# Windowed attention in whole units of eight heads, with scores merged into 128 columns, ahead of two feed-forward layers

## Chip, cores and metric

One Trainium2 chip, one core. The metric is the device time of one execution in microseconds (us). Matrix products run on TensorE (PE), everything else on VectorE (DVE), ScalarE (ACT) and GpSimd (POOL); loads and stores are issued by SyncE (SP).

## What is computed

Three layers follow each other, on 1152 tokens (2 sequences of 576) of 512 numbers:

```python
# 1: attention, 8 heads of 64, window of 128 keys, a bias by distance for each head
scores = scale * np.matmul(q, k.transpose(0, 1, 3, 2))
mask = (rel >= 0) & (rel < window)            # rel = query position - key position
scores = np.where(mask, scores + slopes * -abs(rel), -1e9)
attn = softmax(scores); x = attn @ v          # heads side by side: x is [1152, 512]
# 2: four experts
for e in range(4):
    out += p[:, e:e+1] * (np.maximum(x @ w1[e], 0.0) @ w2[e])   # 512 -> 1024 -> 512
# 3: one more layer
h = out @ w_in                                 # 512 -> 2048
result = (h * np.cos(h)) @ w_out               # 2048 -> 512
```

## The kernel before

Every float32 operand of layers 2 and 3 is split into a high and a low part (`hi`, `lo`), and a product is three passes of matmuls over them. Layers 2 and 3 are done in 12 groups g of 512 hidden features: 0 to 7 are the experts (two each), 8 to 11 the last layer; between groups 7 and 8, at the turn, `flip` transposes the layer's output on PE into the next x. Of the 1152 tokens two thirds go in pairs (`pair`, seven products of 384 columns with sums of operands, T1 to T4, S1 to S4, that `transform` and `first_sums` prepare on ACT, DVE and POOL), the last third by `plain`. `layer2(g, t)` multiplies one tile of 128 tokens by the group's second weights, twelve matmuls, and DVE adds the result into `acc`.

Attention works on 10 units (b, i), the blocks of queries of the two sequences: the first of each has 64 rows, the others 128. A unit is done in two halves of four heads, so there are 20 steps, and step k does the scores of half k (`att_scores`), the sums and normalisation of half k-1, the transposes of half k-3 and the value products of half k-4 (`LAG`). A block of queries sees its own block of keys and the one before, so scores are up to 256 wide: PE writes them to PSUM, DVE adds the bias `bm` and takes the minimum (L362, with the scores' sign turned), ACT takes the exponential (L367) and their sum, DVE inverts it (L376, L377), POOL multiplies (L383), PE transposes both key blocks of each head, eight transposes for a half (L405), DVE and ACT copy them out as `pt` (L415, L417), and PE multiplies by the values of both blocks (L433). A finished unit's x is split (`split_x`, L333, for the last third of the tokens) or transformed (L278 to L313, for the others).

All of this stands in the program in the order in which it is written (`tc.manual_schedule()`), and every engine runs its own instructions in that order. The function `fill(k, s)` puts other work between attention's parts: one `next(jobs)` is a piece of the splitting of weights (an ACT copy and a POOL subtraction of 128x512, or two POOL sums `sm`), `plain` halves are the first group's products, `move(n)` takes n stages of a waiting transform. When a job is through with a raw weight tile it issues the load of the next one (`loads_ahead`, L145, two buffers `raw`) on SP, where the loads of the units stand too (`load_units_to`, L120 to L122).

PSUM has eight banks. During attention `ps1` has two of them for products, the scores three, the transposes two, x one. Afterwards `mm` has six, and `bank()` takes `ps1` for every fourth product. In the groups, `run` goes through `steps(g)`: each entry is a product with the number of stages, jobs and conversions of the last layer's weights (`cv`) that follow it, and at a group's end all waiting transforms are finished.

Of the kernel before, what the change touches and what calls it, by code (L numbers as in the profile page):

```python
# [24 lines left out]
WIN = 128  # L25
# [20 lines left out]
LAG = 3  # L46


@with_exitstack
def tile_kernel(ctx, tc, qT, kT, v, probs, w1, w2, w_in, w_out, out):  # L50
# [13 lines left out]
    ps1 = pool("ps1", bufs=2, space=PSUM)  # L64
# [7 lines left out]
    ptp = ap("ptp", bufs=4)  # L72
    stp = ap("stp", bufs=6)
    ps_s = ap("ps_s", bufs=3, space=PSUM)
# [5 lines left out]
    scr = ppool.tile([128, 4, 256], F32, name="scr", tag="p")  # L80
    bm = mkp.tile([128, H, 256], BF16, name="bm")

    def constants():
        rel_i, rel, msk = scr[:, 0].bitcast(I32), scr[:, 1], scr[:, 2]
        nc.gpsimd.iota(rel_i, pattern=[[-1, 256]], base=WIN, channel_multiplier=1)
        nc.vector.tensor_copy(rel, rel_i)
        nc.gpsimd.memset(msk, 0.0)
        big = -8.0e9
        nc.gpsimd.affine_select(
            out=msk, in_=msk, pattern=[[-1, 256]], compare_op=ALU.is_ge, fill=big,  # L90
            base=WIN, channel_multiplier=1,
        )
        nc.gpsimd.affine_select(
            out=msk, in_=msk, pattern=[[1, 256]], compare_op=ALU.is_ge, fill=big,
            base=-1, channel_multiplier=-1,
        )

        for h in range(H):
            slope = 2.0 ** (-8.0 * (h + 1) / H)
            nc.vector.scalar_tensor_tensor(  # L100
                out=bm[:, h, :], in0=rel, scalar=-8.0 * slope, in1=msk,
                op0=ALU.mult, op1=ALU.add,
            )
        make_identity(nc, ident)


    k_t, q_t, v_t = {}, {}, {}

    def load_unit(b, i):
# [13 lines left out]
        q_t[b, i], v_t[b, i] = qt, vt  # L123

# [215 lines left out]
    def att_scores(u, g):  # L340
# [3 lines left out]
        wid = s0 + n - k0  # L344
        c0 = WIN if i == 0 else 256 - wid
        ps = [ps_s.tile([128, 2, 256], F32, name="s_ps", tag="s_ps") for _ in range(2)]
        for m in range(2):
            for hh in range(2):
                r = slice(64 * hh, 64 * hh + 64)
                nc.tensor.matmul(  # L350
                    ps[hh][:n, m, :wid], q_t[u][r, 2 * g + m, :n],
                    k_t[b][r, 2 * g + m, k0 : s0 + n], start=True, stop=True,
                )
        p = ppool.tile([128, 4, 256], F32, name="p", tag="p")
        nmax = stp.tile([128, 4], F32, name="nmax", tag="nmax")
        den = dens[:, (2 * units.index(u) + g) % 4]
        rec = stp.tile([128, 4], F32, name="rec", tag="rec")
        for m in range(2):
            for hh in range(2):
# [3 lines left out]
                    out=p[:n, k, :wid], in0=ps[hh][:n, m, :wid], in1=bm[:n, h, c0 : c0 + wid],  # L363
# [4 lines left out]
                    out=p[:n, k, :wid], in_=p[:n, k, :wid], func=AF.Exp, scale=-1.0,  # L368
                    bias=nmax[:n, k : k + 1], accum_out=den[:n, k, 0:1],
                )  # L370
        state[u, g] = p, den, rec, wid
# [7 lines left out]
    def att_normalise(u, g):  # L379
        n = UNITS[u[1]][1]  # L380
        p, den, rec, wid = state[u, g]
        for s in (slice(0, 4),) if u[0] == 0 else (slice(0, 2), slice(2, 4)):
            nc.gpsimd.tensor_tensor(  # L383
                out=p[:n, s, :wid], in0=p[:n, s, :wid],
                in1=rec[:n, s].unsqueeze(2).to_broadcast([n, s.stop - s.start, wid]), op=ALU.mult,
            )
        state[u, g] = p

    def key_blocks(i):
        o = 0  # L390
# [291 lines left out]
    with tc.manual_schedule():  # L682
# [13 lines left out]
        def fill(k, s):  # L696
# [5 lines left out]
            if (k, s) == (11, 0):  # L702
                routing()
# [145 lines left out]
```

## Time and profile before

| | us |
|---|---|
| median of 3 runs | 669.71 |
| lowest, highest | 668.44, 672.1 |
| the profiled execution | 668.45 |
| its span in the trace | 666.7 |
| PE, weight loads on PE (PEld) busy | 645.6, 568.7 |
| DVE, ACT, POOL busy | 432.8, 335.9, 367.6 |

The profile shows one execution. Attention takes the first 88.2 us of the span, the pairs of group 0 begin there; the turn lies around 440 to 490, the four groups of the last layer after it. In a timeline, us of start are counted from the span's start, and a bracket gives the engine's idle time just before the instruction and what ended it. Instructions of one engine overlap at their ends, so the distance between two starts, not the duration, is what one costs in a row.

### The profile page before, as it was taken

Reading aid. Unit: us, or ns where it says so; the run is one execution under the profiler, and the core shown is the slowest. Engines: PE = TensorE matmul, PEld = TensorE weight load, DVE = VectorE, ACT = ScalarE, POOL = GpSimd, SP = SyncE. Lnnn points to the kernel's source line nnn. Section 1 sums busy time; section 2 is a strip of 40 time slices with the busy share of each in tenths; the row PEclk is TensorE's granted clock in tenths of the full one; section 3 lists DMA queues with packets and bytes.
Section 4 is the critical chain, followed back from the end, with each engine's and each line's share of the span. In section 5 each row is a group of like instructions: output and inputs, shape, how many; then the busy total and the mean of one; then the engine's idle time right before and its main releaser. Section 6 shows DMA issues by size and latency. Waiting matters only on the chain.

```text
span 666.7 us, 9755 instructions
## 1 busy us (share of the span) xinstructions
PE 645.6 (97%) x3516; PEld 568.7 (85%) x3516; DVE 432.8 (65%) x842; ACT 335.9 (50%) x768; POOL 367.6 (55%) x346
## 2 busy tenths in 40 slices
PE   8989899999999999999999999999799999999997
PEld 5677698998998998988988988988788988988976
DVE  7676776878668578589578562647663563563562
ACT  6878644453344354354343341346684674584560
POOL 3977729356265175183282381465468558558530
PEclk8999999999999999999999999999899999999999
DMA  9162114435417335245236130030101101202002
GB/s 262 41 204 83 32 33 138 130 112 200 128 35 225 106 101 185 79 139 193 80 131 200 32 121 7 32 96 0 33 0 64 65 0 63 65 0 64 17 31 94
DMA packets 39727, 60.40 MB, mean 91 GB/s; under 512 B 5632, under 2 KB 22016, under 8 KB 39680
## 3 DMA queue, kind: packets, MB, share of 16 engines
q1 hardware_dynamic: 39680, 59.80, 28.2%
q8 instruction: 27, 0.44, 0.3%
q14 instruction: 20, 0.16, 0.1%
HBM read 49.04 MB, written 10.75 MB: 90 GB/s over the span
## 4 chain that ended last, share of the span: by engine, by line
PE 78%; DVE 7%; ACT 7%; POOL 4%; issue 2%; DMA 1%; SPq 0%; ACTq 0%; DVEq 0%; POOLq 0%
PE o_ps L631 39%; PE o_ps L537 21%; PE o_ps L565 13%; PE s_ps L350 2%; DVE u L509 2%; ACT r L507 2%; ACT u L506 2%; PE x_ps L433 1%; POOL p L383 1%; POOL w1t L130 1%; PE t_ps L405 1%; POOL hpair L130 1%; DVE o_ps L580 1%; DVE xs L130 1%; DVE u L515 1%
## 5 line engine op out<-in xcount | busy, mean ns | idle before, releaser
L631 PE MATMUL o_ps<-w2t,hpair 128*128 128x512 f32 x864 | 207.3, 392 | 4.3 <-POOL hpair L130 4.1
L631 PEld LDWEIGHTS o_ps<-w2t,hpair 128*128 128x128 f32 x864 | 160.7, 188 | 38.3 <-POOL hpair L130 5.8
L537 PE MATMUL o_ps<-xs,w1t 128*128 128x384 f32 x1008 | 182.5, 338 | 3.9 <-DVE c L580 1.8
L537 PEld LDWEIGHTS o_ps<-xs,w1t 128*128 128x128 f32 x1008 | 177.1, 189 | 7.6 <-DVE c L580 3.1
L130 POOL TENSOR_TENSOR w2t<-raw,w2t 128x512 fp32r<-128x512 f32 x48 | 66.2, 1394 | 82.1 <-ACT w2t L185 82.1
L130 POOL TENSOR_TENSOR w1t<-raw,w1t 128x512 fp32r<-128x512 f32 x48 | 65.0, 1364 | 83.2 <-ACT w1t L155 83.0
L565 PE MATMUL o_ps<-xq,w1t 128*128 128x384 f32 x576 | 110.3, 338 | 0.0
L565 PEld LDWEIGHTS o_ps<-xq,w1t 128*128 128x128 f32 x576 | 101.6, 188 | 3.3
L631 PE MATMUL o_ps<-w2t,h 128*128 128x512 f32 x432 | 103.3, 392 | 0.0
L631 PEld LDWEIGHTS o_ps<-w2t,h 128*128 128x128 f32 x432 | 80.7, 188 | 16.1 <-issue 0.2
L130 POOL TENSOR_TENSOR w1t<-sm,w1t 128x512 fp32r<-128x512 f32 x48 | 64.6, 1356 | 41.9 <-ACT w1t L155 35.1
L509 DVE SCALAR_TENSOR_TENSOR u<-r,u 128x384 f32<-128x384 f32 x48 | 34.6, 726 | 51.7 <-ACT r L507 51.7
L130 POOL TENSOR_TENSOR hpair<-u,hpair 128x384 fp32r<-128x384 f32 x32 | 33.6, 1066 | 42.3 <-ACT hpair L517 42.3
L245 ACT ACTIVATE cr<-cr 128x512 f32<-128x512 f32 x32 | 21.6, 675 | 43.4 <-DVE cv L239 43.4
L367 ACT ACTIVATE p<-p,nmax 128x256 f32<-128x256 f32 (+2 forms) x80 | 36.2, 454 | 13.0 <-DVE nmax L362 12.8
L646 DVE SCALAR_TENSOR_TENSOR accpair<-o_ps,pr,accpair 128x512 f32<-128x512 f32 x42 | 31.3, 745 | 17.3 <-PE o_ps L631 17.3
L233 ACT ACTIVATE cr<-cr 128x512 int32<-128x512 uint32 x32 | 21.6, 675 | 40.7 <-DMA cr<-w_in 25.3
L524 ACT ACTIVATE hpair<-o_ps 128x384 fp32r<-128x384 f32 x48 | 23.4, 488 | 36.6 <-DVE o_ps L580 35.9
L155 ACT ACTIVATE w1t<-sm 128x512 fp32r<-128x512 f32 x48 | 30.0, 627 | 20.3 <-POOL sm L130 20.3
L525 DVE SCALAR_TENSOR_TENSOR hpair<-o_ps,hpair 128x384 fp32r<-128x384 f32 x48 | 26.6, 555 | 20.3 <-ACT hpair L524 20.3
L383 POOL TENSOR_TENSOR p<-p,rec 128x512 f32<-128x512 f32 (+5 forms) x30 | 32.6, 1102 | 9.5 <-DVE rec L377 5.6
L239 DVE SCALAR_TENSOR_TENSOR cv<-cr,cv 128x512 int32<-128x512 int32 x32 | 35.1, 1097 | 1.1
(100 smaller groups left out, 821.3 us busy)
## 6 DMA issues: line engine op xcount, KB each, us to landing
raw<-w SPq DMA_DIRECT2D x32, 512.0 KB, 3.7
cr<-w_in SPq DMA_DIRECT2D x16, 512.0 KB, 4.6
cr<-w_out SPq DMA_DIRECT2D x16, 512.0 KB, 4.5
wi<-cv SPq DMA_DIRECT2D x16, 256.0 KB, 3.6
wo<-cv SPq DMA_DIRECT2D x16, 256.0 KB, 2.3
raw<-wi SPq DMA_DIRECT2D x8, 512.0 KB, 3.5
raw<-wo SPq DMA_DIRECT2D x8, 512.0 KB, 3.5
qt<-qT SPq DMA_DIRECT2D x8, 256.0 KB, 4.9
```

The costliest lines, as they stand in the source:

```text
L130: eng.tensor_tensor(out=out, in0=a, in1=b, op=ALU.subtract)
L155: nc.scalar.activation(out=hi[:, s], in_=src[:, s], func=AF.Copy)
L239: nc.vector.scalar_tensor_tensor(out=a, in0=hw, scalar=-0x40000000, in1=o, op0=ALU.bitwise_and, op1=ALU.bitwise_or,)
L367: nc.scalar.activation(out=p[:n, k, :wid], in_=p[:n, k, :wid], func=AF.Exp, scale=-1.0, bias=nmax[:n, k : k + 1], accum_out=den[:n, k, 0:1],)
L383: nc.gpsimd.tensor_tensor(out=p[:n, s, :wid], in0=p[:n, s, :wid], in1=rec[:n, s].unsqueeze(2).to_broadcast([n, s.stop - s.start, wid]), op ...
L509: nc.vector.scalar_tensor_tensor(out=u, in0=r, scalar=MAGIC, in1=u, op0=ALU.subtract, op1=ALU.subtract)
L524: nc.scalar.activation(out=hi, in_=src, func=AF.Relu)
L525: nc.vector.scalar_tensor_tensor(out=lo, in0=src, scalar=0.0, in1=hi.bitcast(F32), op0=ALU.max, op1=ALU.subtract)
L537: nc.tensor.matmul(ps, w(a, k, m), xs[:, bb, b, m], start=(start and m == 0 and (a, bb) == PASSES[0]), stop=(stop and m == 1 and (a, bb) = ...
L565: nc.tensor.matmul(ps, w(a, 2 * (q % 2) + d // 2, d % 2), xq[:, bb, d], start=(d == 0 and (a, bb) == PASSES[0]), stop=(d == ND - 1 and (a, ...
L631: nc.tensor.matmul(ps, h0[:, a, f, t * 128 : (t + 1) * 128] if t < NQ else hpair[:, a, f, (t - NQ) * 128 : (t - NQ + 1) * 128], w_t[2, g, ...
L646: nc.vector.scalar_tensor_tensor(out=o, in0=ps, scalar=s, in1=o, op0=ALU.mult, op1=ALU.add)
```

## The change

A step is now a whole unit: the scores of both halves, then in between the rest of older units. In program order, for unit k: scores of both halves; sums and normalisation of half 0; value products of unit k-2; `fill`; transposes of half 0 of unit k-1; `fill`; sums and normalisation of half 1; transposes of half 1 of unit k-1; `fill`.

A query sees exactly 128 keys, and of each column of the two key blocks only one is in the window: the one before for a key that is later in its block than the query is in its own. So `copy_predicated` (DVE) lays the older block's scores over the newer one's where the mask `later` says so, and the bias, exponential, normalisation and transposes are done on 128 columns. For the value products a masked copy `po` (pt times `own`) is made, and the result is `ahead` times pt plus `vd` times po, where `ahead` are the older block's values and `vd` the difference of the two, a POOL subtraction for each unit (`values`).

```diff
-    ps1 = pool("ps1", bufs=2, space=PSUM)
+    ps1 = pool("ps1", bufs=1, space=PSUM)
-    ptp = ap("ptp", bufs=4)
+    ptp = ap("ptp", bufs=2)
+    vdp = ap("vdp", bufs=3)
-    ps_s = ap("ps_s", bufs=3, space=PSUM)
+    ps_s = ap("ps_s", bufs=4, space=PSUM)
...
     def load_unit(b, i):
+        if i == 1:
+            nc.sync.dma_start(out=va[64:], in_=v[b, :64, :])
+    def values(b, i):
+        ahead = va if i == 1 else v_t[b, i - 1]
+        vd = vdp.tile([128, DM], F32, name="vd", tag="vd")
+        nc.gpsimd.tensor_tensor(out=vd, in0=v_t[b, i], in1=ahead, op=ALU.subtract)
+        v_d[b, i] = ahead, vd
...
     def att_scores(u, g):
+        if i:
+            for hh in range(2):
+                nc.vector.copy_predicated(
+                    ps[hh][:n, :, 128 + c0 :], later.bitcast(U32)[:n, :, c0:], ps[hh][:n, :, c0:128]
+                )
...
-                    out=p[:n, k, :wid], in0=ps[hh][:n, m, :wid], in1=bm[:n, h, c0 : c0 + wid],
+                    out=p[:n, k, :n], in0=ps[hh][:n, m, 128 : 128 + n], in1=bm[:n, int(i > 1), h, :n],
...
     def att_normalise(u, g):
-        for s in (slice(0, 4),) if u[0] == 0 else (slice(0, 2), slice(2, 4)):
...
+        nc.gpsimd.tensor_tensor(
+            out=p[:n, :, :n], in0=p[:n, :, :n],
+            in1=rec[:n].unsqueeze(2).to_broadcast([n, 4, n]), op=ALU.mult,
+        )
+        if g == 0 and u[1]:
+            values(*u)
     def att_transpose(u, g):
+        for k in range(4):
+            nc.tensor.transpose(tp[:n, k, :n], p[:n, k, :n], ident[:n, :n])
+        nc.scalar.activation(out=pt[:n, :, :n], in_=tp[:n, :, :n], func=AF.Copy)
+            nc.vector.tensor_tensor(
+                out=po, in0=tp, in1=own.unsqueeze(1).to_broadcast([128, 4, 128]), op=ALU.mult
+            )
     def att_pv(u, g):
+                nc.tensor.matmul(o, ahead[:, hs], pt[:, k], start=True, stop=False)
+                nc.tensor.matmul(o, more[:, hs], po[:, k], start=False, stop=True)
...
     def attention(fill):
+        for k in range(n):
+            load_units_to(k + 2)
+            at(k, att_scores, 0)
+            at(k, att_scores, 1)
+            at(k, att_sums, 0)
+            at(k, att_normalise, 0)
+            at(k - 2, att_pv, 0)
+            at(k - 2, att_pv, 1)
             fill(k, 0)
+            at(k - 1, att_transpose, 0)
             fill(k, 1)
+            at(k, att_sums, 1)
+            at(k, att_normalise, 1)
+            at(k - 1, att_transpose, 1)
             fill(k, 2)
...
     def bank():
-        return ps1 if mm is None or count[0] % 4 == 0 else mm
+        return ps1 if mm is None or count[0] % 8 == 0 else mm
...
         def fill(k, s):
-            if s == 0 and 4 <= k < 20:
+            if s and 2 <= k < 10:
                 next(jobs)
-            move(24 if (k, s) == (23, 2) else 2 * (s > 0))
+            move(24 if (k, s) == (11, 1) else 4 if k >= 10 else 2)
...
-    mm = pool("mm", bufs=6, space=PSUM)
+    mm = pool("mm", bufs=7, space=PSUM)
...
     def steps(g):
-            yield layer2(g, 1), 2, 2 if turn else int(not last), 2
-            yield layer2(g, 2), 2, 2 if turn else int(not last), 2
+            yield layer2(g, 1), 2, 2 if turn else int(early), 2
+            yield layer2(g, 2), 2, 2 if turn else int(early), 2
...
-        njobs = 0 if last else 4 if turn else 6 if early else 10
+        njobs = [1] * 10
...
+        elif not last:
+            njobs = [0, 1, 2, 2, 1, 2, 1, 1, 1, 1]
     def run(groups):
-                move(2)
+                move(2 if ncv or stages != 1 else 1)
-            while moved:
-                move(24)
```

The constants change with it (`later`, `own`, the two biases `bm`), the plain halves of group 0 move to units 6 to 9, and three tiles `layer2(0, 0..2)` to the steps behind the last unit. For groups 0 to 7 the number of jobs at each step stays.

On SP, the loads around the first weight load of the second kind (raw of 128x2x512, which waits for a buffer that the sums `sm` give back); the three rows behind it are the loads of unit 6. Before:

```order
L120 DMA qt<-qT 128x4x64
L121 DMA kt<-kT 128x4x64
L122 DMA vt<-v 64x512
L145 DMA raw<-w 128x2x512
L120 DMA qt<-qT 128x512
L121 DMA kt<-kT 128x4x128
L122 DMA vt<-v 128x512
```

And after:

```order
L141 DMA qt<-qT 128x4x64
L142 DMA kt<-kT 128x4x64
L143 DMA vt<-v 64x512
L176 DMA raw<-w 128x2x512
L141 DMA qt<-qT 128x512
L142 DMA kt<-kT 128x4x128
L143 DMA vt<-v 128x512
L147 DMA va<-v 64x512
```

The order is the same; only the load of `va` came in behind.

On DVE, the end of attention: the transform of the last unit (tx, xk and xs) and behind it the first step of the first pair product, u. acc is the eviction of a second-layer tile. Before:

```order
L644 TENSOR_SCALAR acc_129<-o_ps,pr 128x512
L130 TENSOR_TENSOR xs<-xk,xs 128x2x128
L130 TENSOR_TENSOR xk<-xk,tx 128x2x128
L130 TENSOR_TENSOR xs<-xk,xs 128x2x128
L130 TENSOR_TENSOR tx<-x_ps,xk 128x256
L130 TENSOR_TENSOR tx<-x_ps,tx 128x256
L130 TENSOR_TENSOR xk<-x_ps,xk 128x256
L130 TENSOR_TENSOR xs<-xk,xs 128x2x128
L130 TENSOR_TENSOR xs<-tx,xs 128x2x128
L130 TENSOR_TENSOR xs<-xk,xs 128x2x128
L644 TENSOR_SCALAR acc_129<-o_ps,pr 128x512
L580 TENSOR_TENSOR u_1328<-o_ps,p_1319 128x384
```

After:

```order
L682 TENSOR_SCALAR acc_135<-o_ps,pr 128x512
L161 TENSOR_TENSOR tx<-x_ps,xk 128x256
L161 TENSOR_TENSOR tx<-x_ps,tx 128x256
L161 TENSOR_TENSOR xk<-x_ps,xk 128x256
L161 TENSOR_TENSOR xs<-xk,xs 128x2x128
L161 TENSOR_TENSOR xs<-tx,xs 128x2x128
L161 TENSOR_TENSOR xs<-xk,xs 128x2x128
L161 TENSOR_TENSOR xk<-xk,tx 128x2x128
L161 TENSOR_TENSOR xs<-xk,xs 128x2x128
L682 TENSOR_SCALAR acc_135<-o_ps,pr 128x512
L618 TENSOR_TENSOR u_1288<-o_ps,p_1279 128x384
```

The last eviction stands behind the whole transform of the last unit in both; the rest of the transform before it has moved ahead of the second-last eviction.

On POOL, the turn: xs<-accpair are low parts of the transformed x, h and hpair low parts of the hidden layer, w2t and w1t those of weights. Before:

```order
L130 TENSOR_TENSOR xs<-accpair,xs 128x2x128 x2
L130 TENSOR_TENSOR h_128<-u,h_128 128x384
L130 TENSOR_TENSOR w2t<-raw,w2t 128x512 x2
L130 TENSOR_TENSOR h_128<-u,h_128 128x384
L130 TENSOR_TENSOR hpair<-u,hpair 128x384 x4
L130 TENSOR_TENSOR w1t<-raw,w1t 128x512 x2
L130 TENSOR_TENSOR hpair<-u,hpair 128x384 x2
L130 TENSOR_TENSOR w1t<-raw,w1t 128x512
L130 TENSOR_TENSOR hpair<-u,hpair 128x384 x2
L130 TENSOR_TENSOR w1t<-raw,w1t 128x512
```

After:

```order
L161 TENSOR_TENSOR xs<-accpair,xs 128x2x128
L161 TENSOR_TENSOR h_134<-u,h_134 128x384
L161 TENSOR_TENSOR w2t<-raw,w2t 128x512 x2
L161 TENSOR_TENSOR xs<-accpair,xs 128x2x128
L161 TENSOR_TENSOR h_134<-u,h_134 128x384
L161 TENSOR_TENSOR hpair<-u,hpair 128x384 x4
L161 TENSOR_TENSOR w1t<-raw,w1t 128x512 x2
L161 TENSOR_TENSOR hpair<-u,hpair 128x384 x4
L161 TENSOR_TENSOR w1t<-raw,w1t 128x512
L161 TENSOR_TENSOR h_134<-u,h_134 128x384
L161 TENSOR_TENSOR w1t<-raw,w1t 128x512
```

The last low part of x has moved behind the two w2t steps, and the third w1t step, which stood between hpair's low parts, behind all of them.

## Rows read from the trace of the kernel before

**Rows 1.** Windows: us, busy us (count) PE PEld DVE ACT POOL, clock, DMA, GB/s

```profile
0.00:88.20 88.20, 80.27 (x685) 60.18 (x686) 62.50 (x270) 65.96 (x231) 60.30 (x67) 0.98 0.40 122
...
476.50:480.20 3.70, 3.70 (x12) 3.70 (x13) 2.19 (x4) 2.71 (x6) 3.29 (x3) 0.55 0.15 46
```

**Rows 2.** Chain of waits, 0 to 160: start us, us, what

```profile
32.15 1.42 POOL sm L130 x2
...
33.59 0.38 SPq L145
...
34.55 4.30 DMA kt<-kT
...
42.10 1.02 PE x_ps L433 x16
...
62.25 1.06 PE s_ps L350 x8
...
63.32 1.02 PE t_ps L405 x8
...
85.41 2.94 PE o_ps L631 x12
```

**Rows 3.** Timeline of DVE, attention: start us, us, instruction, idle before

```profile
19.51 0.42 DVE L362 CUSTOM_DVE_ANT_0 p<-s_ps,bm 128x256 f32<-128x256 f32 x1
...
26.59 0.69 DVE L130 TENSOR_TENSOR xq<-x_ps,xq 128x512 fp32r<-128x512 f32 x1 [1.87 <-ACT xq L333]
27.19 0.42 DVE L362 CUSTOM_DVE_ANT_0 p<-s_ps,bm 128x256 f32<-128x256 f32 x1
...
28.57 0.16 DVE L376 TENSOR_REDUCE rec<-dens 128x4 f32<-128x8 f32 x1
...
28.85 0.66 DVE L415 COPY pt<-t_ps 128x512 f32<-128x512 f32 x1
...
33.78 0.20 DVE L362 CUSTOM_DVE_ANT_0 p<-s_ps,bm 64x64 f32<-64x64 f32 x1
...
40.09 0.34 DVE L362 CUSTOM_DVE_ANT_0 p<-s_ps,bm 128x192 f32<-128x192 f32 x1
...
63.45 0.42 DVE L362 CUSTOM_DVE_ANT_0 p<-s_ps,bm 128x256 f32<-128x256 f32 x1
...
91.25 0.75 DVE L644 TENSOR_SCALAR acc<-o_ps,pr 128x512 f32<-128x512 f32 x1
```

**Rows 4.** Groups by line and shape: busy us, mean ns, idle before

```profile
L383 POOL TENSOR_TENSOR p<-p,rec 128x512 f32<-128x512 f32 x12 | 12.4, 1057 | 0.7 <-DVE rec L377 0.7
...
L367 ACT ACTIVATE p<-p,nmax 128x256 f32<-128x256 f32 x48 | 23.8, 498 | 6.5 <-DVE nmax L362 6.4
...
L367 ACT ACTIVATE p<-p,nmax 64x64 f32<-64x64 f32 x16 | 5.3, 335 | 4.8 <-DVE nmax L362 4.8
...
L130 DVE TENSOR_TENSOR accpair<-accpair,tx 128x256 f32<-128x256 f32 x3 | 2.6, 859 | 0.1
...
L130 DVE TENSOR_TENSOR tx<-x_ps,xk 128x256 f32<-128x256 f32 x3 | 1.3, 425 | 0.7 <-ACT xk L286 0.7
```

**Rows 5.** Timeline of ACT, unit 4 and the end of attention

```profile
25.96 0.59 ACT L333 ACTIVATE xq<-x_ps 128x512 fp32r<-128x512 f32 x1
27.65 0.51 ACT L367 ACTIVATE p<-p,nmax 128x256 f32<-128x256 f32 x1 [1.10 <-DVE nmax L362]
...
85.52 0.60 ACT L286 ACTIVATE xk<-x_ps 128x512 f32<-128x512 f32 x1
```

**Rows 6.** Waits of PE, 430 to 667: us in total, times, longest

```profile
PE o_ps L631 <- POOL hpair L130: 4.1, 4, 1.4
...
PE o_ps L537 <- ACT p L586: 1.7, 1, 1.7
```

**Rows 7.** Timeline of PE at the turn

```profile
476.50 3.91 PE L537 MATMUL o_ps<-xs,w1t 128*128 128x384 f32 x12 [1.31 <-DVE c L580]
```

**Rows 8.** Timeline of POOL at the turn

```profile
475.99 2.52 POOL L130 TENSOR_TENSOR w2t<-raw,w2t 128x512 fp32r<-128x512 f32 x2
```

More of the change, by code (lines that the diff above doesn't have):

```diff
@@ new lines, in tile_kernel @@
+    own = mkp.tile([128, 128], F32, name="own")
+    va = mkp.tile([128, DM], F32, name="va")
+    bm = mkp.tile([128, 2, H, 128], BF16, name="bm")
+    def constants():
+        rel_i = own.bitcast(I32)
+        nc.gpsimd.iota(rel_i, pattern=[[-1, 128]], base=0, channel_multiplier=1)
+        nc.gpsimd.memset(later, 0.0)
+        nc.gpsimd.affine_select(
+            out=later, in_=later, pattern=[[0, 2], [-1, 128]], compare_op=ALU.is_ge, fill=float(WIN),
+            base=0, channel_multiplier=1,
+        )
@@ L86, in constants @@
         nc.vector.tensor_copy(rel, rel_i)
-        nc.gpsimd.memset(msk, 0.0)
-        big = -8.0e9
+        nc.vector.tensor_tensor(out=rel, in0=rel, in1=later[:, 0], op=ALU.add)
+        nc.gpsimd.memset(edge, 0.0)
         nc.gpsimd.affine_select(
-            out=msk, in_=msk, pattern=[[-1, 256]], compare_op=ALU.is_ge, fill=big,
-            base=WIN, channel_multiplier=1,
-        )
+            out=edge[:, :64], in_=edge[:, :64], pattern=[[-1, 64]], compare_op=ALU.is_ge, fill=-8.0e9,
+            base=0, channel_multiplier=1,
+        )
@@ new lines, in constants @@
+        for e in range(2):
+            for h in range(H):
+                slope = 2.0 ** (-8.0 * (h + 1) / H)
+                if e == 0:
+                    nc.vector.scalar_tensor_tensor(
+                        out=bm[:, e, h], in0=rel, scalar=-8.0 * slope, in1=edge,
+                        op0=ALU.mult, op1=ALU.add,
+                    )
+                else:
+                    nc.gpsimd.tensor_scalar(
+                        out=bm[:, e, h], in0=rel, scalar1=-8.0 * slope, scalar2=None, op0=ALU.mult
+                    )
+            if e == 0:
+                make_identity(nc, ident)
@@ L93, in constants @@
+        nc.gpsimd.memset(va[:64], 0.0)
+        nc.gpsimd.memset(own, 1.0)
         nc.gpsimd.affine_select(
-            out=msk, in_=msk, pattern=[[1, 256]], compare_op=ALU.is_ge, fill=big,
-            base=-1, channel_multiplier=-1,
-        )
[L98 to L103, printed above, removed]
@@ L104, in constants @@
-        make_identity(nc, ident)
-    k_t, q_t, v_t = {}, {}, {}
+            out=own, in_=own, pattern=[[1, 128]], compare_op=ALU.is_ge, fill=0.0,
+            base=0, channel_multiplier=-1,
+        )
+    k_t, q_t, v_t, v_d = {}, {}, {}, {}
     def load_unit(b, i):
@@ L455, in tile_kernel @@
     units = [(b, i) for b in range(B) for i in range(len(UNITS))]
-    steps = [(u, g) for u in units for g in range(2)]
     nloaded = [0]
@@ L755, in steps @@
         )
-        njobs = 0 if last else 4 if turn else 6 if early else 10
+        njobs = [1] * 10
         if g == 0:
-            njobs += 2
+            njobs = [2, 2, 1, 1, 1, 1]
+        elif turn:
+            njobs = [1] * 4
+        elif early:
+            njobs = [1] * 6
+        elif not last:
+            njobs = [0, 1, 2, 2, 1, 2, 1, 1, 1, 1]
         for k, o in enumerate(order):
-            more = min(njobs, 2 if g == 0 and k < 2 else 1)
+            more = njobs.pop(0) if njobs and not last and str(o)[0] != "f" else 0
             if isinstance(o, int):
```

131 lines of the change are left out of this document (53 added, 78 removed).

## The prediction

> **What bounds the kernel now.** I read busy times by stage first. In attention (0 to 88.2 us) PE is busy 80.27 us, but its weight loads fill only 60.18, and DVE, ACT and POOL are each busy 60 to 66 [rows 1]: no engine is full. So I went to the chain of waits, which says who ends last. In the middle of attention it is POOL's sums of weights, then SP and one load of keys; only towards the end PE [rows 2]. A unit's cost is therefore a loop through DVE and ACT, which I follow by start-to-start times in the two engines' timelines: units 3, 4, 5 and 6 start on DVE at 19.51, 27.19, 33.78 and 40.09, unit 9 at 63.45 [rows 3]. After 430 us PE's waits stand in one table: 4.1 for hpair in second-layer tiles, 1.7 for a copy p at the turn, where 1.31 more follow for c [rows 6, 7].
>
> A rule bears on this. The Trainium skill (Trainium Kernel Development and Optimization, the advice on reading a trace at its start) holds that matmul busy time is a bad measure of how full PE is, because matmuls are pipelined, and that weight-load busy time is the better one. By it PE has 28 us of room in attention, by its busy time 8; the chain, which names POOL, SP and a DMA, agrees with the rule, and the rule speaks against counting the removed transposes as time (rival E).
>
> **A unit after the change.** Merged scores make an exponential 128 wide. It costs .335 at 64 and .498 at 256 [rows 4]; on that line .39. Eight are 3.12. DVE's bias-and-minimum step costs .345 at 256 (four in 27.19 to 28.57) [rows 3]; at 128 between half and all of that, .21 as an estimate. The merge, copy_predicated over 256 elements a partition out of and into PSUM, is not in this trace. Bounds: .35 (a 425 ns subtract of that size from PSUM, whose successor starts about .07 before its end) and .86 (the slowest DVE step of that size) [rows 4]; a gain is excluded, since it is an added instruction. I take .35, from the row with PSUM. Two stand at the head of each half.
> The loop, as DVE and ACT run it in program order: two merges .70; first step to first exponential .33 (.46 at 256: 27.19 to 27.65, less the step's .13) [rows 3, 5]; eight exponentials 3.12; ACT's high part of x to DVE's low part .63 (25.96 to 26.59) [rows 3, 5]; that low part .60 (26.59 to 27.19), two products po at .60 each, sums .28 (28.57 to 28.85) [rows 3]. Sum .70+.33+3.12+.63+.60+1.20+.28 = 6.86. It was 7.7 (19.51 to 27.19) and 6.6 (27.19 to 33.78) [rows 3]. So **units 2 to 5 win next to nothing**: eight narrower exponentials give .8, the merges and the masked product take it back. PE's lost work (64 transposes), its new order and POOL's halved normalisation lie under this loop, of which PE needs about 5 (scores 2.1, transposes 1, value products 2 [rows 2]) and half a product. Unit 0's sums now stand behind all eight exponentials, about 1 later; by unit 5 both versions are level again, unit 4 near 26.7, unit 5 near 33.4.
>
> **Unit 6's keys.** On SP the loads of unit 6 stand behind a weight load raw, before and after. That load waits for POOL's sums of weights (two in 1.42, ending at 33.57); SP goes on at 33.59, the keys land at 38.85 [rows 2]. After, POOL does in unit 4: a normalisation 1.06 [rows 4], the new subtraction vd, two sums .71 each, a normalisation, two sums. vd (128x512) lies between that 1.06 and 1.26, a w2t subtraction of the size [rows 4, 8]; I take 1.26. That is 6.2, begun once DVE has done four merges, eight steps and the sums (1.40+1.68+.28 = 3.36 into the unit). 26.7+3.36+6.2 = 36.3, **+2.7**; the same 5.3 us through SP and DMA put the keys at 41.6. PE has idled for some us by then. At the turn, after gaps, twelve products took 3.91 at a granted clock of .55 (its 1.2 GHz level), 1.8 over full clock [rows 1, 7]; half as much work here, **+.8**.
> Units 6 to 8 took 23.4 (40.09 to 63.45) [rows 3]; after, three loops 20.6, .4 for their share of half products on ACT and DVE, .7 for unit 8's keys behind the next weight load: 21.7, **-1.7**.
>
> **The end of attention.** From unit 9's scores to the first pair product it took 26.1 (62.25 to 88.35) [rows 2]. After: scores 1.06; DVE 3.36 as above; POOL's normalisation 1.06, vd 1.26, a w2t step 1.26, a low part .7, normalisation 1.06; four transposes .5; six hand-overs of .05 (25.96+.59 to 26.59): 10.6. Then value products 2.05, a second-layer tile 2.9, .75 for the one bank's eviction, a tile 2.9, value products 2.05. Now ps1 is one bank instead of two, and the pair's first product, the eighth counted, takes it. It must wait until DVE has evicted the third tile, and that eviction stands behind the whole transform of unit 9 (DVE's order, in the change's section). Before it stood there too, at 91.25, and nobody waited, since the product took the other bank. ACT's copy of x to the eviction's end: 85.52 to 92.0, 6.5 [rows 3, 5]. Sum 27.8, **+1.7**. PE idles 3.6 of it; I charge a clock fall like the turn's, **+1.8**.
>
> **Turn and late groups.** The flush at a group's end goes. At the turn PE waited 1.7 for a copy queued behind it, 1.31 for the next step, and then lost 1.8 to its clock [rows 1, 6, 7]. After, the copy is in time, but on POOL a low part (xs<-accpair) stands behind two w2t steps (2.52) [rows 8], and the product that needs it waits about 2.1. Gain 3.0+1.8 less 2.1 = 2.7 with the clock kept, .9 without, up to 4.8 if that low part is early after all; I take **-2.7**, since half a wait less may leave the clock alone.
> In groups 8 to 11 second-layer tiles wait for hpair's low part on POOL, 4.1 in four places, at most 1.4 [rows 6]; in 8 to 10 a w1t subtraction stands ahead of it, which the new table of jobs moves behind it. Ends: nothing and 3.4 (the 4.1 less group 11's share, some .7). I take **-2.8**, since the step ahead is as long (1.26 [rows 8]) as the wait. In the main loop PE comes back to a bank after eight products either way, so bank() costs nothing there.
>
> **Sum.** 2.7+.8-1.7+1.7+1.8 = +5.3 in attention, -5.5 after it: -.2 on the profiled 668.45 us (span 666.7). The runs' median, 669.71, is 1.26 above that execution. Forecast **669.5**.
>
> **Rivals.**
> B, slower: PE's clock falls in units 2 to 5, where PE would idle about 1.8 of 6.9 us in one stretch. Its 5 us at half speed are 10, 3.2 over the loop; in two units +6.4: 675.9. It decides once a fall lasts longer than a unit's PE work. For it the turn, where gaps of 1.7 and 1.3 were enough [rows 6, 7]; against it, that PE in attention is busy 80 of 88 us now [rows 1]. Chance .14.
> C, slower: copy_predicated costs .86. Two on the loop of seven units (the eighth waits for keys): 14 x .51 = +7.1, 676.6. For it, two operands in PSUM; against, the row of .425 with one [rows 4]. It decides from about .6. Chance .12.
> D, faster: POOL has the sums of weights done in time (unit 4 starts sooner, or jobs fall into POOL's gaps) and unit 6's keys come as before: -3.5, 666.0. Chance .20.
> E, faster: PE was the bound after all; 64 transposes at .128 (1.02 for eight [rows 2]) are won and the tail's stall isn't there: -8.2-3.5, 657.8. For it, 80 of 88 us; against, the chain's names. Chance .09.
> F, the change doesn't do what it says at the turn: PE's clock falls there as before, 671.3. Chance .12.
> The forecast, 666 to 672.5 by the ends of its own terms: .33.
>
> **How the numbers follow.** The range takes in the forecast, D and F and most of B's and C's lower halves: 663.5 to 676; E and their upper halves stay out. About .5% (3.35 us) is what a measurement here can tell from no change. Faster by more: E, most of D, the forecast's low end, .30. Slower by more: B, C and a little of F, .28. Within: .42.
>
> **What would show it.** Right: units 2 to 5 on DVE 6.8 to 7.0 apart; unit 6's scores waiting for kt till after 41; a PE gap of 3 to 4 us, named after DVE's acc, just ahead of the first pair product; no wait for hpair in groups 8 to 10. Wrong: copy_predicated above .6, with exponentials waiting for it; scores of unit 6 before 40; a granted clock under .9 from 13 to 40 us.

## The result, and the profile after

The changed kernel takes 679.57 us (median of 4 runs, 678.41 to 681.21) against 669.69 before: ratio 1.0133, 95% interval 1.0105 to 1.0162. It is 9.9 us slower by the medians, 8.9 by the ratio; the forecast was 669.5 in 663.5 to 676. The profiled execution took 679.5 us, its span is 677.8, 11.1 above the span before, whose execution (668.45) is near the fastest of its kernel.

PE's timeline shows where it happened. The bracket is PE's idle time ahead of the row and what ended it:

```profile
43.27 2.67 PE L380 MATMUL s_ps<-kt,qt 64*128 64x192 f32 x16 [4.87 <-DMA kt<-kT]
...
59.51 2.90 PE L380 MATMUL s_ps<-kt,qt 64*128 64x256 f32 x16 [2.25 <-DVE po L436]
...
68.25 2.00 PE L380 MATMUL s_ps<-kt,qt 64*128 64x256 f32 x16
...
76.80 0.63 PE L430 MATMUL t_ps<-ident,p 128*128 128x128 f32 x4 [1.45 <-DVE po L436]
79.72 1.12 PE L430 MATMUL t_ps<-ident,p 128*128 128x128 f32 x4 [2.30 <-POOL p L417]
...
89.32 3.01 PE L669 MATMUL o_ps<-w2t,h 128*128 128x512 f32 x12 [1.85 <-DVE acc L682]
...
100.96 16.41 PE L575 MATMUL o_ps<-xs,w1t 128*128 128x384 f32 x84 [3.72 <-DVE acc L682]
...
490.31 3.57 PE L575 MATMUL o_ps<-xs,w1t 128*128 128x384 f32 x11 [1.81 <-POOL xs L161]
...
561.90 3.94 PE L669 MATMUL o_ps<-w2t,hpair 128*128 128x512 f32 x16 [0.17 <-POOL hpair L161]
```

And before the change, the scores of unit 6 and the first pair:

```profile
38.98 0.92 PE L350 MATMUL s_ps<-kt,qt 64*128 64x192 f32 x8 [0.78 <-DMA kt<-kT]
...
88.19 14.75 PE L537 MATMUL o_ps<-xs,w1t 128*128 128x384 f32 x84
```

The rows after are the scores of units 6, 8 and 9, the two halves of the last unit's transposes, the second of the three tiles, the first pair, the turn and a late group. The profile puts unit 8's wait down to DVE's po, which the scores do not read; they read the keys, whose load is issued at 54.85 and takes 4.4 to 5.2 us to land, so this is a wait for keys as well. Against before, each stretch between two such marks became longer or shorter by (the first three rows give the us at which the stretch ends, the fourth how long it takes):

| stretch | before | after | change | forecast |
|---|---|---|---|---|
| to the scores of unit 6 | 38.98 | 43.27 | +4.3 | +2.7 |
| to the scores of unit 9 | 62.25 | 68.25 | +1.7 | -.9 |
| to the first pair product | 88.35 | 100.96 | +6.6 | +1.7 |
| 84 pair products | 14.6 | 16.4 | +1.8 | +1.8 |
| the turn, up to group 8's second pair | | | -.8 | -2.7 |
| groups 8 to 11 | | | -2.5 | -2.8 |

The forecast's -.9 is its -1.7 for units 6 to 8 and +.8 for the clock. The changes add up to 11.1, where the forecast's own sum is -.2. Of these 11.3 us, 9.1 lie in attention and 1.9 at the turn. The main loop has not moved: from the end of the first pair to the turn's first long wait (102.78 to 458.84 before, 117.21 to 473.27 after) it takes 356.06 us in both.

The windows behind the long gaps name a second part of the loss. Columns as in [rows 1]; the third number from the end is the granted clock:

```profile
33.60:36.50 2.90, 2.84 (x24) 2.63 (x26) 2.48 (x20) 1.51 (x10) 2.82 (x5) 0.50 0.04 8
43.20:46.80 3.60, 3.54 (x26) 3.13 (x27) 2.18 (x17) 1.41 (x7) 0.00 (x0) 0.55 0.86 253
59.50:64.20 4.70, 4.69 (x35) 4.05 (x37) 3.70 (x23) 2.57 (x14) 2.47 (x3) 0.64 0.45 136
79.70:84.40 4.70, 4.67 (x36) 4.05 (x36) 2.32 (x3) 0.60 (x1) 2.93 (x3) 0.50 0.44 112
100.90:104.20 3.30, 3.24 (x12) 3.27 (x13) 0.00 (x0) 0.49 (x1) 0.00 (x0) 0.61 0.00 0
490.30:493.70 3.40, 3.39 (x12) 3.39 (x13) 2.60 (x4) 1.94 (x5) 1.24 (x1) 0.56 0.46 154
```

Six times PE went to its 1.2 GHz level for most of a stretch, each time after gaps. In the last five it worked on the path that sets the end; the first lies under the wait for the keys.

The units themselves behave as worked out. DVE's timeline, the first merge of units 3 and 4, the first bias step of unit 5, and the eviction that the first pair waits for:

```profile
21.37 0.75 DVE L390 COPY_PREDICATED s_ps<-later,s_ps 128x256 f32<-128x256 uint32 x2
...
28.14 0.75 DVE L390 COPY_PREDICATED s_ps<-later,s_ps 128x256 f32<-128x256 uint32 x2
...
34.88 0.21 DVE L397 CUSTOM_DVE_ANT_0 p<-s_ps,bm 64x64 f32<-64x64 f32 x1
...
100.07 0.74 DVE L682 TENSOR_SCALAR acc<-o_ps,pr 128x512 f32<-128x512 f32 x1
```

Units 3 to 5 stand 6.77 and 6.74 apart, where 6.86 was forecast (unit 2, whose low part of x is half as wide, to unit 3 is 6.54: 14.83 to 21.37); but units 3, 4 and 5 stand 1.9, .95 and 1.1 later than in [rows 3], not level. The groups by shape give the three prices that were guessed:

```profile
L402 ACT ACTIVATE p<-p,nmax 128x128 f32<-128x128 f32 x64 | 24.8, 388 | 13.1 <-DVE nmax L397 13.1
...
L390 DVE COPY_PREDICATED s_ps<-later,s_ps 128x256 f32<-128x256 uint32 x24 | 9.0, 423 | 0.8 <-PE s_ps L380 0.8
L153 POOL TENSOR_TENSOR vd<-vt 128x512 f32<-128x512 f32 x6 | 7.7, 1277 | 0.0
```

An exponential of 128 takes .388 (.39 forecast), a merge 423 ns, two of them .66 to the next start (.70 forecast), vd 1.28 (1.26 forecast).

The keys of unit 6, in the timelines of POOL (the last sum of weights) and of SP (the weight load behind it, and the keys):

```profile
37.08 0.72 POOL L161 TENSOR_TENSOR sm<-raw,sm 128x256 f32<-128x256 f32 x1
```

```profile
37.83 0.37 SPq L176 DMA_DIRECT2D raw<-w  x1
...
38.76 0.42 SPq L142 DMA_DIRECT2D kt<-kT  x1
```

The sums end at 37.8 (36.3 forecast, 33.57 before), SP goes on at once, and from there to the scores it takes 5.4 us as before.

### The profile page after: what moved, and what is told of

It reads as the page before. It is cut to its first block, busy times and chain, and to the rows that moved or that the text cites. A ratio compares the mean times of both kernels' runs of the same rounds, so it can differ in the third digit from the quotient of the medians.

```text
span 677.8 us, 9698 instructions
## 1 busy us (share of the span) xinstructions
PE 643.6 (95%) x3452; PEld 571.0 (84%) x3452; DVE 435.9 (64%) x867; ACT 329.7 (49%) x764; POOL 367.3 (54%) x356
## 4 chain that ended last, share of the span: by engine, by line
PE 77%; DVE 9%; ACT 8%; POOL 3%; issue 2%; DMA 1%; DVEq 0%; SPq 0%; ACTq 0%; POOLq 0%
PE o_ps L669 37%; PE o_ps L575 21%; PE o_ps L603 13%; ACT p L402 2%; DVE u L547 2%; PE x_ps L459 1%; ACT r L545 1%; ACT u L544 1%; PE s_ps L380 1%; PE x_ps L460 1%; POOL hpair L161 1%; DVE xs L161 1%; DVE u L553 1%; PE t_ps L430 1%; DVE o_ps L618 1%
## 5 line engine op out<-in xcount | busy, mean ns | idle before, releaser
L575 PE MATMUL o_ps<-xs,w1t 128*128 128x384 f32 x1008 | 184.6, 340 | 7.4 <-DVE acc L682 3.7
L547 DVE SCALAR_TENSOR_TENSOR u<-r,u 128x384 f32<-128x384 f32 x48 | 38.8, 816 | 61.0 <-ACT r L545 59.6
L186 ACT ACTIVATE w1t<-sm 128x512 fp32r<-128x512 f32 x48 | 30.0, 627 | 34.3 <-POOL sm L161 34.3
L402 ACT ACTIVATE p<-p,nmax 128x128 f32<-128x128 f32 (+1 forms) x80 | 30.1, 377 | 19.9 <-DVE nmax L397 19.9
L551 ACT ACTIVATE u<-u 128x384 f32<-128x384 f32 x48 | 24.7, 518 | 18.4 <-DVE u L547 18.3
```

Of the source, the lines that this page charges most:

```text
L186: nc.scalar.activation(out=hi[:, s], in_=src[:, s], func=AF.Copy)
L402: nc.scalar.activation(out=p[:n, k, :n], in_=p[:n, k, :n], func=AF.Exp, scale=-1.0, bias=nmax[:n, k : k + 1], accum_out=den[:n, k, 0:1],)
L547: nc.vector.scalar_tensor_tensor(out=u, in0=r, scalar=MAGIC, in1=u, op0=ALU.subtract, op1=ALU.subtract)
L551: nc.scalar.activation(out=u, in_=u, func=AF.Sin, scale=-TWOPI)
L575: nc.tensor.matmul(ps, w(a, k, m), xs[:, bb, b, m], start=(start and m == 0 and (a, bb) == PASSES[0]), stop=(stop and m == 1 and (a, bb) = ...
```

## Experiments

All times are medians; the kernel before took 669.6 to 670.5 beside each set of runs.

**The keys.** Loads of units 6 to 9 one unit earlier, and nothing else:

```diff
-            load_units_to(k + 2)
+            load_units_to(k + 2 if k < 4 else k + 3)
```

> The changed kernel, only the loads of units 6 to 9 issued one unit earlier, so that on SP they stand ahead of the weight loads that wait for POOL's sums. Theory (late keys hold units 6 and 8, and the gaps also halve PE's clock behind them): scores of units 6 and 8 wait for no kt; unit 6 starts on DVE near 41.2 instead of 44.6, unit 9's scores near 61.5 instead of 68.3, about 7 us less in all (672.5 on the medians). Rival (the DVE and ACT loop and POOL's jobs hold these units anyway): no kt wait, but under 2 us less (677.5 or more).

Measured 672.24, 7.3 less than the changed kernel (ratio to before 1.0032, 1.0017 to 1.0048). PE's timeline, scores of units 6 and 9, and the first pair:

```profile
39.69 1.59 PE L380 MATMUL s_ps<-kt,qt 64*128 64x192 f32 x16
...
59.02 2.00 PE L380 MATMUL s_ps<-kt,qt 64*128 64x256 f32 x16
...
93.32 16.37 PE L575 MATMUL o_ps<-xs,w1t 128*128 128x384 f32 x84 [3.73 <-DVE acc L682]
```

No wait for keys is left, and from unit 6 to unit 9 it takes 19.3 us instead of 25.0 (23.3 before). The late keys, with the clock behind them, cost 7.3 us: the theory holds. Unit 9's scores start 9.2 sooner, more than was expected, but the end of attention takes 1.6 longer (34.3 from there to the pair, 32.7 in the changed kernel): the last unit's first transposes now wait 3.06 for DVE's po instead of 1.45. The pair still waits 3.73.

**The bank.** The one bank of ps1 given to another product of the eight:

```diff
-        return ps1 if mm is None or count[0] % 8 == 0 else mm
+        return ps1 if mm is None or count[0] % 8 == 7 else mm
```

> The changed kernel, only ps1 given to the seventh product of each eight instead of the eighth, so that the first pair product takes a bank of mm. Theory (the wait of 3.72 us before the pair, and the half clock behind it, come from that one bank alone): the wait goes, the 84 matmuls of the first pair products take 14.6 us instead of 16.4, 5.4 us less in all (674.2). Rival (the pair also needs what ACT, DVE or POOL do behind unit 9's transform): the wait comes back one product later, at p1 or at u, 2 us less at most.

Measured 673.70, 5.9 less (1.006, 1.0032 to 1.0088). PE's timeline, the third tile and the pair behind it:

```profile
95.22 3.02 PE L669 MATMUL o_ps<-w2t,h 128*128 128x512 f32 x12
...
98.07 14.75 PE L575 MATMUL o_ps<-xs,w1t 128*128 128x384 f32 x84
```

No gap stands between them, and 84 products take 14.75 instead of 16.41. This term was forecast at 3.6 and 1.8, and that is about what it is. The pair starts only 2.9 sooner in this trace, because the clock fell behind the second tile here (twelve matmuls in 4.29 us behind a wait of 1.87), as it had not in the changed kernel (3.01 behind 1.85).

**The clock.** Extra matmuls ahead of the scores of units 6 and 8, so that the waits stay and PE has work in them:

```diff
+        if g == 0 and b == 1 and i in (1, 3):
+            for _ in range(WAIT[i]):
+                nc.tensor.matmul(ps[0][:, 0, :128], ident, ident, start=True, stop=True)
```

> The changed kernel with 36 and 16 extra matmuls of 128 columns (their result is overwritten by the scores) ahead of the scores of units 6 and 8, where PE waits 4.87 and 2.25 us for keys: the waits stay, PE is busy in them. If PE's clock falls because of these gaps, the granted clock stays at 1.0 behind both, scores of unit 6 take 2.0 instead of 2.67 us, of unit 8 2.0 instead of 2.9, and the value products behind them also run at full speed: 2.5 to 3.5 us less in all. If the clock has another cause, no gain, or a loss of up to 1 us where the extra matmuls outlast the wait.

Measured 681.30, 1.7 more. The 36 extra matmuls took 8.2 us, longer than the wait of 4.87, and held unit 6 up until 46.75, so this run could not give the time back. It was done again with fewer:

> As warm_waits, with 20 and 8 extra matmuls, since one of them took .228 us there (36 took 8.20 and outlasted the keys by 3.5). If PE's half clock comes from its gaps: unit 6's scores start at 43.3 as in the changed kernel but take 1.6 us, unit 7's start 1.6 us sooner, near 49.9, and unit 8's take 2.0; 2 to 3.5 us less in all. If the clock is not the cost, unit 7's scores start at 51.5 as before.

Measured 677.95, 1.6 less than the changed kernel (1.0119, 1.0098 to 1.0140). That is under the 2 to 3.5 expected, and the two intervals overlap, so the time alone decides nothing; the trace does. In the profile, PE's timeline with the extra matmuls and the scores of units 6, 7 and 8, and the window behind the first wait:

```profile
38.64 4.63 PE L380 MATMUL s_ps<-ident 128*128 128x128 f32 x40
43.49 1.57 PE L384 MATMUL s_ps<-kt,qt 64*128 64x192 f32 x16 [0.22 <-DMA kt<-kT]
...
50.17 2.00 PE L384 MATMUL s_ps<-kt,qt 64*128 64x256 f32 x16
...
58.96 2.07 PE L384 MATMUL s_ps<-kt,qt 64*128 64x256 f32 x16 [1.27 <-DMA kt<-kT]
```

```profile
43.20:46.80 3.60, 3.38 (x49) 3.05 (x48) 2.36 (x19) 1.59 (x9) 0.01 (x1) 1.00 0.93 269
```

At the same late keys the granted clock is 1.00 instead of .55, 49 instructions are done in the window where 26 were, and unit 7 starts 1.35 sooner (50.17 for 51.52). So it is the gap, not the work behind it, that halves the clock here. From unit 6's scores to unit 7's it takes 6.68 instead of 8.25, from unit 8's to unit 9's 7.10 (66.06) instead of 8.74: 1.6 us each for the clock. Not all of it reaches the end, since unit 8 still waits for its keys: its scores start .55 sooner, unit 9's 2.2. Here the profile names the wait of unit 8 as DMA kt.

**PE as the bound.** Every transpose twice:

```diff
-            nc.tensor.transpose(tp[:n, k, :n], p[:n, k, :n], ident[:n, :n])
+            for _ in range(2):
+                nc.tensor.transpose(tp[:n, k, :n], p[:n, k, :n], ident[:n, :n])
```

> The changed kernel with every transpose of attention done twice (80 more instructions on PE, some 10 us of PE work). Theory (attention is a loop through DVE and ACT, PE has room): under 2 us more, or even a little less where PE's gaps are filled and its clock stays up. Rival (PE is the bound of attention, and the removal of transposes was worth their time): 7 to 10 us more.

Measured 679.38, .2 less than the changed kernel. With an interval of 1.0087 to 1.0161 the rival's 7 to 10 us are excluded: PE's waits take up the 80 transposes (4.87 becomes 3.75, 2.25 becomes .71, 1.45 becomes .61). So PE is not the bound of the changed attention, and rival E falls with it; that the 64 removed transposes were worth nothing in the kernel before too is concluded from that, not tried there. The rule of the Trainium skill (Trainium Kernel Development and Optimization, the advice on reading a trace), to go by the weight loads' busy time, agrees with this run.

**The loop of a unit.** The sums and normalisation of a unit's second half behind the next unit's first four bias steps:

```diff
             at(k, att_scores, 0)
+            at(k - 1, att_sums, 1)
+            at(k - 1, att_normalise, 1)
             at(k, att_scores, 1)
...
-            at(k, att_sums, 1)
-            at(k, att_normalise, 1)
             at(k - 1, att_transpose, 1)
```

> The changed kernel, only the sums and normalisation of a unit's second half moved into the next unit, behind its first four bias steps. Theory (a unit's 6.77 us on DVE are a loop: DVE waits for the last exponentials before it may begin the next unit's steps, and ACT then waits for DVE): units 2, 3 and 4 come 5.7 to 6.2 us apart. The keys of unit 6 then still hold the attention, so that in all 1 to 4 us are gained. Rival (ACT, POOL or PE are full at 6.8 us a unit): units stay 6.6 us or more apart.

Measured 681.50, 1.9 more. DVE's timeline, first steps of units 2 to 5:

```profile
13.25 0.76 DVE L390 COPY_PREDICATED s_ps<-later,s_ps 128x256 f32<-128x256 uint32 x2 [0.63 <-PE s_ps L380]
...
20.06 0.75 DVE L390 COPY_PREDICATED s_ps<-later,s_ps 128x256 f32<-128x256 uint32 x2
...
27.06 0.75 DVE L390 COPY_PREDICATED s_ps<-later,s_ps 128x256 f32<-128x256 uint32 x2
...
33.78 0.21 DVE L397 CUSTOM_DVE_ANT_0 p<-s_ps,bm 64x64 f32<-64x64 f32 x1
```

6.81, 7.00 and 6.72 apart: the rival holds. PE's timeline names what comes next, the second half's transposes that wait for a normalisation now done later on POOL:

```profile
23.19 0.66 PE L430 MATMUL t_ps<-ident,p 128*128 128x128 f32 x4 [1.32 <-POOL p L417]
```

The start does gain: unit 2 begins at 13.25 instead of 14.83, since its steps no longer wait for unit 1's last exponentials. But the forecast's 6.86, right to .1, was not the only chain of that length, and the run does not say which of POOL, ACT and PE binds at 6.8. Nor did the 1 to 4 us come that were expected in all. The early start lasts up to unit 9's scores (63.68, 4.6 sooner), and all of it goes at the end, where the last unit's second transposes, at 79.08, wait 4.70 for POOL instead of 2.30.

**Together.** Keys, bank and sums, then keys and bank alone:

> The changed kernel with the keys loaded early, the pair's first product moved off ps1 and the second sums moved into the next unit, all three at once. If the three causes are what makes attention slow, the gains add: 7 + 5.4 + 2 to 4 less, 663 to 665, below the kernel before by .7 to 1%. If something else takes over (POOL's jobs, the transposes at the end), 668 to 672.

> The changed kernel with the keys loaded early and the pair's first product off ps1, without the sums moved. keys_early gave 7.3 less and pair_bank 5.9 less; if the two causes are separate the sum is 13.2 less, 666.4, and 2 us less than keys_bank_sums. If the waits overlap, 668 or more.

Measured 668.35 (.9979, .996 to .9998) and 666.83 (.9953, .9935 to .9971). Keys and bank give 12.7 less, of 13.2 if they added fully; with the sums moved, 1.5 of it goes, as in the run of the sums alone, though the two intervals overlap. The trace shows the same cause: the last unit's second transposes wait 5.16 for POOL.

**The last unit.** On top of keys and bank, for the last unit alone the second normalisation ahead of the pieces of weight splitting:

```diff
             fill(k, 0)
+            if k == n - 1:
+                at(k, att_sums, 1)
+                at(k, att_normalise, 1)
             at(k - 1, att_transpose, 0)
             fill(k, 1)
-            at(k, att_sums, 1)
-            at(k, att_normalise, 1)
+            if k < n - 1:
+                at(k, att_sums, 1)
+                at(k, att_normalise, 1)
```

> keys_bank, and for the last unit alone the sums and normalisation of its second half ahead of the two pieces of weight splitting. Theory (the last unit's transposes wait 2.3 us for that normalisation, which stands on POOL behind a w2t step of 1.28 and a low part of .9, and PE's clock halves behind the two gaps): transposes of the last half some 2 us sooner, 2 to 4 us less than keys_bank (662.5 to 664.5). Rival (DVE, which then waits for the last exponentials in front of other work, gives it back): within 1 us of keys_bank.

Measured 664.97 (.9924, .9902 to .9946), 1.9 less than keys and bank. PE's timeline, last transposes and first pair:

```profile
70.33 1.08 PE L430 MATMUL t_ps<-ident,p 128*128 128x128 f32 x4 [0.73 <-DVE po L436]
...
87.67 7.64 PE L579 MATMUL o_ps<-xs,w1t 128*128 128x384 f32 x43
```

The last transposes wait .73 for DVE instead of 2 us for POOL and start 1.3 sooner, the two tiles behind them 1.0 and 1.1. The pair begins at 87.67, 2.7 before that of keys and bank (90.35). The other 1.6 is the clock behind the second tile, in keys and bank and then in this kernel:

```profile
80.98 4.23 PE L669 MATMUL o_ps<-w2t,h 128*128 128x512 f32 x12 [1.90 <-DVE acc L682]
```

```profile
79.91 3.01 PE L673 MATMUL o_ps<-w2t,h 128*128 128x512 f32 x12 [1.53 <-DVE acc L686]
```

So POOL's order was the cause of the wait, but it is worth about 1.1 us in the trace, not 2 to 4. That the edit also keeps the clock up is not shown: the next kernel has the same attention, and there it fell (4.47 behind a wait of 1.86). The intervals of keys and bank with and without the edit overlap.

**Behind attention.** The kernel before with the new table alone, with the flush gone alone, and with both; the edits are those of the change's `steps` and `run`.

> The kernel before with only the new table of jobs of groups 8 to 10. By the trace of the changed kernel the waits for hpair in three groups go from 3.4 to .3 us: 3.0 to 3.4 less in all (ratio .9952). If the .4 us that the second pair of groups 10 and 11 took longer in the changed kernel comes with the table, 2.3 less.

> The kernel before with only the flush at each group's end taken away and the transforms' stages moved one at a time in single steps. Theory (one wait is traded for another: the copy p is in time, but a low part of x stands behind two w2t steps on POOL, and PE's clock falls all the same): 1 us less in all, a wait for POOL xs of about 1.8 us and a product run at half clock behind it. The prediction's own term was 2.7 less.

> The kernel before with the new table of jobs and without the flush, so the whole change behind attention and nothing of it in attention. late_table and no_flush gave 1.9 and 2.0 us less, each with an interval of about 1.5 us. If they add, 665.5 to 666.5 (ratio .994 to .996): then attention and the pair behind it cost the change 13 to 14 us, and the repaired attention (keys_bank_norm, 665.0) is worth no more than the old one. If late_table and no_flush share a gain, 667.5 to 668: then the repaired attention is 2 to 3 us better than the old one.

Measured 667.80 (.9971, .9945 to .9998), 668.22 (.9969, .9949 to .9989) and 666.14 (.9939, .9922 to .9957). By the ratios the table alone gives 1.9 us, where 3.0 to 3.4 was expected (2.3 with longer second pairs), and the flush alone 2.0, where 1 was; each interval is wide enough to hold the expected number. Together they give 4.1, so they add. PE's timeline, a wait for hpair with the table alone, and the turn with the flush gone alone:

```profile
549.38 3.96 PE L631 MATMUL o_ps<-w2t,hpair 128*128 128x512 f32 x16 [0.15 <-POOL hpair L130]
```

```profile
476.85 3.15 PE L537 MATMUL o_ps<-xs,w1t 128*128 128x384 f32 x11 [1.81 <-POOL xs L130]
```

So the part behind attention is worth 4.3 us by the medians and 4.1 by the ratio, and attention with the pair behind it costs the change about 14. The repaired attention, 664.97, and the old one under the same rest, 666.14, can't be told apart (.9902 to .9946 and .9922 to .9957).

**The turn.** On top of keys, bank and normalisation, the two w2t steps two products later:

```diff
-                    more = g > 0 and 1 <= k <= 2
+                    more = g > 0 and (3 <= k <= 4 if g == NG1 else 1 <= k <= 2)
```

> keys_bank_norm, and the two w2t steps at the turn moved two products later, behind the low part of x that PE waits 1.81 us for. Theory (that wait and the half clock behind it are POOL's order alone): 1.8 for the wait and up to 1.6 for the clock, 2 to 3.4 us less than keys_bank_norm, 660 to 662. Rival (the next thing, DVE's c or its low part T4, is as late): under 1 us.

Measured 664.72 (.9917, .9898 to .9936), .25 below the kernel without it, with overlapping intervals: not the 2 to 3.4 of the theory. PE's timeline, where the low part was waited for, and the second pair:

```profile
474.13 2.52 PE L579 MATMUL o_ps<-xs,w1t 128*128 128x384 f32 x12 [0.40 <-ACT h L559]
...
484.86 3.63 PE L579 MATMUL o_ps<-xs,w1t 128*128 128x384 f32 x18 [1.26 <-ACT p L628]
```

The wait for POOL is gone, so the order was its cause, and a new one of 1.26 stands at the next pair's copy p on ACT; that copy is neither of the two that the rival named. The granted clock is 1.00 behind both (474.1 to 476.5 and 484.8 to 488.4), where the kernel without the edit is at .50 from 475.5 to 478.5. From the first product at the turn to the end of the second pair it takes 20.73 us instead of 22.28, 1.55 less. One reason why the time does not show it is in the trace: this execution came to the turn .98 later, because its clock fell behind the second tile and its first pair started at 88.65 instead of 87.67.

This last kernel is the fastest that was run, .8% below the kernel before; against the one without the turn's edit it is level.

## Why the prediction was wrong

The step that failed is the sum for attention with the first pair: +5.3 was forecast, and by the same marks it is +14.4. Its two main waits, for unit 6's keys behind POOL's sums and for the one bank before the pair, were named rightly. Four of its terms were too small: the start of unit 4, units 6 to 8 with late keys, the way from unit 9's scores to the end of its value products, and the clock behind the new waits.

**The units: right in size.** 6.86 against 6.77 and 6.74, a merge at .33 to the next start, the exponential at .39. Rival C is out. That nothing is won by the narrower scores in units 2 to 5 was right too. That the loop through DVE and ACT alone sets the 6.8 is not: sums_later took a link out of it, and the period stayed. The agreement to .1 is in that part luck.

**The start, mis-sized.** "About 1 later; by unit 5 level" was 1.9 at unit 3 and 1.1 at unit 5, and unit 4 began at 28.14, not 26.7. The forecast's own numbers did not give 26.7: 1 later at unit 3 (20.5) and two loops of 6.86 put units 4 and 5 at 27.4 and 34.2. And 1.6 of the 1.9 stands ahead of the first score already, at a place that the forecast put at nothing. PE's first rows before:

```profile
1.18 3.78 PE L688 MATMUL o_ps<-warm 128*128 128x256 f32 x8 [1.18 <-DVE dens L686]
4.90 0.90 PE L350 MATMUL s_ps<-xk,qt 64*64 64x64 f32 x10
```

And after:

```profile
1.51 5.06 PE L726 MATMUL o_ps<-warm 128*128 128x256 f32 x8 [1.51 <-DVE dens L724]
6.50 1.12 PE L380 MATMUL s_ps<-xk,qt 64*64 64x64 f32 x16
```

The four warm-up matmuls at the start (two records each) write to ps1. With one bank instead of two each waits for the one before it, .78 us three times, and the first scores, behind them on PE, begin at 6.50 instead of 4.90. This is read from the trace; no run gave the warm-up another bank, so how much of it reaches unit 4 is not shown, but 28.14 less 1.6 is close to the forecast's 26.7.

The 1.4 by which unit 4 is late goes straight through POOL's chain, which was rightly sized (37.8 less 28.14 is 9.66, forecast 9.6), to the keys: +4.3 instead of +2.7. keys_early shows that the mechanism is the one that the prediction named. Rival D, the keys as early as before, is out.

**Units 6 to 8: the wrong sign.** The forecast took three loops, .4 and .7 for unit 8's keys, and .8 for the clock. Without late keys it is 19.3 (keys_early), so the loops win more than was counted; with them unit 8 waits 2.25 and PE runs twice at half clock, where .8 was counted once. By warm_waits_fit each of the two costs 1.6.

**The end of attention: the largest error.** The bank's wait was forecast and sized rightly (3.6 and 1.8; 3.72 and 1.8; 5.9 in the run that undoes it). What failed is the rest of the sum: 21.3 from the scores of unit 9 to the end of its value products, measured 26.0 (68.25 to 94.3); the transform behind it took 6.4, as forecast. The last transposes start at 79.72, 11.5 after the scores of unit 9 where 10.1 was worked out; behind gaps of 1.45 and 2.30 the clock is at .50 and the last four transposes take 1.05 instead of .5 and eight heads' value products 3.7 (80.77 to 84.44), not 2.05; the one bank's eviction between two tiles costs 1.85, not .75, because it stands on DVE in the middle of a transform. keys_bank_norm shows POOL's order as the cause of the 2.30, worth about 1.1; the rest is read from the trace and was not tried by itself.

**The clock, the common step.** Rival B had the mechanism and the wrong place: it looked at units 2 to 5, where the one fall (33.6 to 36.5) is hidden by the wait for keys. The forecast charged a clock fall behind two gaps in attention and the pair, at .8 and 1.8; there were four that counted, behind new waits of 1.45 and 2.30, 2.25, 3.72 and 4.87 us; the wait of 1.85 at 89.32 brought none (twelve matmuls in 3.01 as at full clock). That a wait of about that length can go either way stands in the last section.

**Turn and late groups.** At the turn the wait for xs was forecast at 2.1 and is 1.81, and the clock fell; the result, -.8, is near the term's lower end (.9), which was rival F. The step that failed here is "half a wait less may leave the clock alone". In groups 8 to 10 the waits for hpair went from 3.4 to .3, a little better than forecast; but the second pairs of groups 10 and 11 became .6 longer each, with a wait for c of .32 instead of .16. Group 10's wait for c, before and after:

```profile
587.19 2.35 PE L537 MATMUL o_ps<-xs,w1t 128*128 128x384 f32 x12 [0.16 <-DVE c L580]
```

```profile
599.19 2.37 PE L575 MATMUL o_ps<-xs,w1t 128*128 128x384 f32 x12 [0.32 <-DVE c L618]
```

That comes with the table, since the run with the table alone has it too (.33); the forecast did not have it. So it is in part luck that -2.5 lies so close to the -2.8: 3.1 was won at hpair and 1.1 lost at the second pairs.

## What to carry to other kernels

Where several stages each leave PE waiting, reckon with a clock fall behind every wait that the change adds or lengthens, not only behind the longest, and look first for a way to fill or to remove the wait. Loads that other work needs soon don't belong on a queue behind a load that waits for a buffer: one line that issued them a unit earlier was worth 7.3 us here. When a pool of banks gets smaller, go through everything that takes a bank from it: here the pair's first product was found, the eviction between two tiles was put too low, and the warm-up was overlooked. A computed period that agrees with the trace is not proof of its chain, since another engine can have the same period; take one link out before building on it.

## What had not been expected of the hardware

A float32 matmul of 128 columns leaves two records in the trace and costs the time of both: the 20 extra ones of warm_waits_fit stand as 40 records in 4.63 us, .23 us for each matmul.

The length of a wait does not tell whether the clock falls behind it. At the turn, behind a wait of 1.80 to 1.81 us in the same place, the next 11 products and the twelve matmuls of the tile behind them took 6.32 us in the changed kernel (3.57 and 3.11 by their rows), 6.32 in no_flush, where the fall only came later (3.15 and 3.54), and 4.78 in all_but_attention, where the clock stayed up (2.18 and 2.92). The tile in no_flush, and the 11 products in all_but_attention:

```profile
479.79 3.54 PE L631 MATMUL o_ps<-w2t,h 128*128 128x512 f32 x12
```

```profile
476.93 2.18 PE L537 MATMUL o_ps<-xs,w1t 128*128 128x384 f32 x11 [1.80 <-POOL xs L130]
```

And behind the wait of 1.85 to 1.90 us ahead of the second tile at the end of attention, the twelve matmuls took 3.01 us in the changed kernel and in warm_waits, but 4.2 to 4.6 in pair_bank, transposes_twice, sums_later, keys_bank, keys_bank_sums and keys_bank_norm_turn. There is one trace of each kernel, so it is not shown whether the kernel or the single execution makes the difference.
